# Two heads' scores on the two row halves of TensorE, and softmax reciprocals by transposes, in a fused attention and MLP kernel

## The chip, the cores and the metric

One NeuronCore of a Trainium2 chip runs the whole program. The metric is the device time of one execution in microseconds (us). Both sides are compared by the median of several executions; beside them stands one profiled execution, from which all rows below are read.

## The reference, cut to what matters

```python
def _attn_ref(q, k, v, f):                      # 4 batches, 8 heads, 576 tokens, head size 64, float32
    scores = np.matmul(q, k.transpose(0, 1, 3, 2)) / np.sqrt(D)
    cum = np.cumsum(np.log(np.clip(f, 0.0001, 1.0)), axis=-1)
    decay = cum[:, :, :, None] - cum[:, :, None, :]
    scores = np.where(causal, -1000000000.0, scores + decay)
    attn = np.exp(scores - np.max(scores, axis=-1, keepdims=True))
    attn = attn / (np.sum(attn, axis=-1, keepdims=True) + 1e-09)
    return np.matmul(attn, v)
...
h = x @ w_in        # 2304 tokens, 512 -> 2048, leaky relu, 2048 -> 512
g = np.maximum(0.01 * h, h)
x = g @ w_out       # then a second MLP of the same sizes with silu
```

The term of the gates `f` that differs along a row of scores is the cumulated logarithm of the key's position. So the kernel adds one row per head, the cumulated gates, to the product of queries and keys.

## The kernel before, in words

The host only lays inputs out. Everything is float32. A float32 matmul of TensorE runs in four passes and shows in the trace as two weight loads and two matmul records; where the kernel uses the one-pass type (`F32R`), an operand is split into a high and a low part, and three one-pass products stand in for one.

The tokens of a batch are cut in two halves: the first 256 tokens (the first half) and the other 320. An attention step is one head of one half, 64 in all, numbered `n`: 0 to 31 are the first halves (8 heads of 4 batches, `plain(n)`), 32 to 63 the second halves, which the change doesn't touch. A first half has two blocks of 128 queries; the first sees 128 keys, the second 256.

For a step of a first half, before the change:
- `load_first` (batch 0) and `load_head` (the others) bring queries and keys of two heads into tiles of 65 partitions. 64 are the head's dimensions, the 65th is a row of ones (queries) or of cumulated gates (keys), sent by DMAs of its own (L180, L683). So one four-pass matmul of 65 rows gives score plus gate.
- `score` (L744) takes a PSUM bank for each block and queues the matmul (`product`, L792); VectorE adds the mask and takes the row's extreme (L772), ScalarE takes the exponential and its sum (L815).
- The first two steps (`n < DIRECT`) are another case: a matmul of 64 rows (L783) and then 128-row products with the triangle `tri` (L785), before and after the change.
- `transp` (L858) transposes the probabilities on TensorE (L886) in a bank of the set `sp` (three banks), and VectorE or ScalarE copies them to SBUF (L379, L380).
- `pair_shares` (L846) adds 1e-9 to a pair's four columns of sums and takes reciprocals (L849, L850), one per query. `weigh` (L938) does a pair of heads at once: `spread` (L959) brings the reciprocals along the free dimension with four matmuls, each a column of `st` broadcast to 64 columns of weights against the identity, into the second half of a bank; `factors` copies them out as `xn` (L379 or L380); `product` (L979) multiplies values by probabilities, the two heads on the two column halves of the array (64 columns each), into the first half of the same bank; L999 multiplies the two, and `to_ring` (L920) writes high and low parts into the ring that feeds the first MLP.

The rest of the kernel is the two MLPs. The first product of the first MLP (L1062, tiles `hps`, `hpw`) runs between the attention steps. Its weights come as words which `conv_in` (L1892, `to_f32` L1837) turns into float32 and splits: one pass of ScalarE and three of VectorE (L1846 to L1850), then a copy and a subtraction. From 350 us on there is only MLP work.

The order of instructions on each engine is written by a planner (`Plan`): it simulates the engines with costs given in the code and queues what has the lowest rank first. Attention has rank 0, the first MLP and its weights rank 1. A matmul of the first MLP fills what attention leaves; before there is one, TensorE is given filler products of zeros (`fillers`, L476 to L486). On the chip, each engine runs its queue strictly in this order and waits where an operand is not ready.

## Time and profile before

| what | us |
|---|---|
| median of 3 executions | 945.29 |
| lowest and highest | 942.88, 946.74 |
| the profiled execution, its time | 945.92 |
| its span from first to last instruction | 944.2 |

Of the span, the first halves' attention takes about the first 85 us, the second halves' reaches to some 350 us. PE is TensorE's matmul side, PEld its weight loads, DVE is VectorE, ACT is ScalarE, POOL is GpSimd; SPq is the queue that issues most DMAs. A matmul's record lasts longer than the array is held by it, since ends are modelled and records overlap; what a matmul costs is read from its start to the start of the next one. In a row of the timeline, the first number is the start and the second the length of the merged records, `x2` their count; `65*128 65x256` means 65 rows of weights by 128 columns, against 256 columns that stream through.

### The profile page before, as it was taken

Reading aid. Unit: us, or ns where it says so; the run is one execution under the profiler, and the core shown is the slowest. Engines: PE = TensorE matmul, PEld = TensorE weight load, DVE = VectorE, ACT = ScalarE, POOL = GpSimd, SP = SyncE. Lnnn points to the kernel's source line nnn. Section 1 sums busy time; section 2 is a strip of 40 time slices with the busy share of each in tenths; the row PEclk is TensorE's granted clock in tenths of the full one; section 3 lists DMA queues with packets and bytes.
Section 4 is the critical chain, followed back from the end, with each engine's and each line's share of the span. In section 5 each row is a group of like instructions: output and inputs, shape, how many; then the busy total and the mean of one; then the engine's idle time right before and its main releaser. Section 6 shows DMA issues by size and latency. Waiting matters only on the chain.

```text
span 944.2 us, 17797 instructions
## 1 busy us (share of the span) xinstructions
PE 936.8 (99%) x6389; PEld 882.4 (93%) x6389; DVE 739.4 (78%) x1715; ACT 593.5 (63%) x1301; POOL 72.0 (8%) x79
## 2 busy tenths in 40 slices
PE   9999999999999999999999999999999999999998
PEld 7777997788898989999999999999999999999998
DVE  5889964988898853889889699848564588888885
ACT  6879965676787863666446477556466764444442
POOL 2002331121331200000000000000000000000000
PEclk9999999999999999999999999999999999999999
DMA  7576634778575618996767685896757774454442
GB/s 196 153 194 205 195 106 137 231 232 260 191 241 188 208 57 298 335 382 199 248 239 233 207 266 187 302 332 228 269 175 245 243 224 121 127 156 140 129 135 67
DMA packets 157524, 195.43 MB, mean 207 GB/s; under 512 B 9222, under 2 KB 142966, under 8 KB 157404
## 3 DMA queue, kind: packets, MB, share of 16 engines
q1 hardware_dynamic: 157004, 193.91, 64.1%
q8 instruction: 50, 0.82, 0.4%
q10 hardware_dynamic: 432, 0.39, 0.1%
q14 instruction: 38, 0.31, 0.1%
HBM read 124.61 MB, written 69.65 MB: 206 GB/s over the span
## 4 chain that ended last, share of the span: by engine, by line
PE 89%; DVE 4%; ACT 3%; DMA 2%; issue 1%; SPq 0%; DVEq 0%; ACTq 0%
PE m L1659 19%; PE m L1801 19%; PE acc L1352 16%; PE hpw L1062 14%; PE sps L792 6%; PE av L979 5%; PE hps L1062 4%; PE tps L886 4%; DMA qk<-in_kt_dram 1%; ACT sc L815 1%; DVE gs L394 1%; PE av L959 1%; DMA x_d<-u 1%; DVE gq L1491 1%; DVE sc L772 1%
## 5 line engine op out<-in xcount | busy, mean ns | idle before, releaser
L1352 PE MATMUL acc<-gs,w 128*128 128x384 f32 x1008 | 181.0, 339 | 1.0 <-DVE gs L394 1.0
L1062 PE MATMUL hpw<-ring,w 128*128 128x320 f32 (+1 forms) x960 | 180.7, 330 | 0.0
L1659 PE MATMUL m<-xc,w 128*128 128x384 f32 x1008 | 180.1, 339 | 0.0
L1801 PE MATMUL m<-w,gc 128*128 128x256 f32 x1512 | 179.9, 281 | 0.0
L1801 PEld LDWEIGHTS m<-w,gc 128*128 128x128 f32 x1512 | 179.7, 188 | 0.0
L1352 PEld LDWEIGHTS acc<-gs,w 128*128 128x128 f32 x1008 | 177.7, 188 | 1.5 <-DVE gs L394 1.4
L1659 PEld LDWEIGHTS m<-xc,w 128*128 128x128 f32 x1008 | 177.7, 188 | 0.6 <-ACT z L1697 0.3
L1062 PEld LDWEIGHTS hpw<-ring,w 128*128 128x128 f32 x960 | 150.0, 188 | 6.9 <-issue 0.7
L379 ACT CAST gc<-g 128x512 fp32r<-128x512 f32 (+1 forms) x180 | 80.6, 490 | 85.7 <-DVE g L1491 47.5
L815 ACT ACTIVATE sc<-sc,st 128x576 f32<-128x576 f32 (+2 forms) x160 | 92.8, 581 | 29.3 <-DVE st L772 26.4
L1285 ACT CAST gs<-gq 128x768 fp32r<-128x768 f32 x84 | 69.5, 836 | 46.6 <-PE acc L1352 24.7
L772 DVE CUSTOM_DVE_ANT_0 sc<-sps,zmask 128x288 f32<-128x288 f32 (+2 forms) x160 | 71.7, 450 | 27.7 <-PE sps L792 17.8
L394 DVE TENSOR_TENSOR gc<-g,gc 128x512 fp32r<-128x512 f32 (+1 forms) x180 | 90.4, 528 | 2.7 <-ACT gc L379 1.5
L394 DVE TENSOR_TENSOR gs<-gq,gs 128x768 fp32r<-128x768 f32 x84 | 79.6, 956 | 12.3 <-ACT gs L1285 12.0
L390 POOL TENSOR_TENSOR m<-qk,m 64x288 fp32r<-64x288 f32 x64 | 67.0, 1066 | 256.3 <-ACT m L379 202.3
L1491 DVE TENSOR_TENSOR g<-g 128x256 f32<-128x256 f32 x144 | 58.9, 422 | 18.0 <-DMA g<-g_d 17.3
L2050 ACT CAST w<-w 128x512 fp32r<-128x512 f32 x84 | 50.9, 620 | 30.4 <-DMA w<-w_d 30.1
L886 PE MATMUL tps<-ident,sc 66*107 66x66 f32 (+3 forms) x480 | 66.4, 268 | 0.3
L394 DVE TENSOR_TENSOR w<-w 128x512 fp32r<-128x512 f32 x84 | 56.2, 689 | 12.6 <-ACT w L2050 12.5
L792 PE MATMUL sps<-m,s 66*128 66x288 f32 (+5 forms) x256 | 63.2, 328 | 0.5 <-DVE st L772 0.3
L886 PEld LDWEIGHTS tps<-ident,sc 66*107 66x107 f32 (+3 forms) x480 | 55.4, 152 | 5.5 <-issue 1.8
L1062 PE MATMUL hps<-ring,w 128*128 128x256 f32 x384 | 56.2, 289 | 0.0
(133 smaller groups left out, 1121.5 us busy)
## 6 DMA issues: line engine op xcount, KB each, us to landing
w<-w_d SPq DMA_DIRECT2D x84, 256.0 KB
gq<-g_d SPq DMA_DIRECT2D x48, 384.0 KB
g_d<-z SPq DMA_DIRECT2D x24, 768.0 KB
g<-g_d SPq DMA_DIRECT2D x36, 512.0 KB
w_d<-f SPq DMA_DIRECT2D x16, 896.0 KB
g_d<-gw SPq DMA_DIRECT2D x32, 320.0 KB
qk<-in_kt_dram SPq DMA_DIRECT2D x32, 288.0 KB
wst<-in_w_dram SPq DMA_DIRECT2D x18, 512.0 KB
```

Source lines behind the costliest of these rows:

```text
L379: ("act", act_cost(n, base), lambda: nc.scalar.copy(dst, src), 0.0),
L394: ("dve", dve_cost(n), lambda: nc.vector.tensor_tensor(dst, a, b, op=ALU.subtract), 0.0),
L772: yield dve(w, lambda: nc.vector.tensor_tensor_reduce(out=sc[0:qn, k0:k0 + w], in0=ps[0:qn], in1=zmask[0:qn, z0:z0 + w], scale=-0.125, sca ...
L792: nc.tensor.matmul(ps[0:qn], ht[x][:, qs], ht[y][:, k0:k0 + w], start=r == 0, stop=r == len(ops) - 1)
L815: yield act(kn, lambda: nc.scalar.activation(sc[0:qn, 0:kn], sc[0:qn, 0:kn], ACTF.Exp, scale=-1.0, bias=st[0:qn, col(a):col(a) + 1], accum ...
L886: nc.tensor.transpose(ps[0:k1 - k0, o:o + qn], ht["p"][i][0:qn, k0:k1], ident[0:qn, 0:qn])
L1062: nc.tensor.matmul(dst, w[:, wi, c * 128:(c + 1) * 128], x(xi, c), start=(first_ and c == 0 and r == 0), stop=(c == KC - 1 and r == 2), sk ...
L1285: yield act(2 * TB, lambda: nc.scalar.copy(t[:, 0], src), 0, 0.09)
L1352: nc.tensor.matmul(dst, w[:, e, wi, j * 128:(j + 1) * 128], x[:, xi, e], start=start and s == 0 and e == 0 and r == 0, stop=stop and s == ...
L1491: ("dve", dve_cost(n), lambda: nc.vector.tensor_tensor(dst, a, b, op=op_), 0.0),
L1659: nc.tensor.matmul(dst, w[:, wi, c * 128:(c + 1) * 128], x[:, xi, c], start=start and c == 0 and r == 0, stop=stop and c == 1 and r == 2, ...
L1801: nc.tensor.matmul(banks[b][:, e], t[:, gi, a * 128:(a + 1) * 128], w[:, wi], start=begin and a == 0 and r == 0, stop=jp == NP // 2 - 1 an ...
```

## The change

It concerns the first halves alone, but for one rank.

- **Loads.** Four heads are loaded together: the even ones of the four on partitions 0 to 63, the odd ones on 64 to 127, no 65th row. The cumulated gates get a tile of their own: for batch 0 one float32 row per head on partition 0 or 64 (`first["row"]`), for the others two rows, high and low part (`gate_rows`), read from `cum_d`. The tensor `cum_p` goes, and `cum_d` is sent in two parts.
- **Scores.** `score_pair` queues a block of both heads at once: two matmuls of 64 rows, one on each row half, then two small ones that add the gates, weights of ones on one row (four passes, batch 0) or on two rows (one pass, the other batches). Each head has one bank for both its blocks: the first in columns 0 to 127, the second in 128 to 383. Banks go back when both blocks have been read.
- **Reciprocals.** They are copied 64 times each (`[128, 4, 64]`, ScalarE or VectorE), and `spread` becomes two plain transposes.
- **Weights.** `to_f32` in `conv_in` goes from rank 1 to rank 0. One slot of the weights' store is held until the last first half is scored.

```diff
+    unity = at["const"].tile([128, 128], F32R, name="unity")
...
+    spare = slot(H // 2 - 1, [128, ROW_BUFS, 2, HALF[0][1]], F32R, "gate_rows")
+    gate_rows = [spare[:, i] for i in range(ROW_BUFS)]
...
+            yield dma(221e3, lambda: nc.sync.dma_start(out=cum_d[:, 1:4], in_=f32(cr)), 0)
             signal("cum_d")
+            yield dma(74e3, lambda: nc.sync.dma_start(out=cum_d[:, 0], in_=f32(cr[:, 0])), 0)
+            signal("cum_1")
...
-        yield wait("ones")
-        yield act(256, lambda: nc.scalar.copy(cf[:, 1], ps[0:H]), 0)
+        yield act(256, lambda: nc.scalar.copy(cf, ps[0:H]), 0)
         signal("cf")
+        row = first["row"]
         yield par(*[seq(
-            dma(8e3, partial(nc.sync.dma_start, out=first[i][64:65], in_=cf[2 * i:2 * i + 2]), i - H),
-            signals(("row", i)),
-        ) for i in range(DIRECT // 2, H // 2)])
+            dma(8e3, partial(nc.sync.dma_start, out=row[64 * e:64 * e + 1], in_=cf[e:H:2]), -1),
+        ) for e in range(2)])
...
+            t = slot(i, [128, 2, 2, tn], F32, "qk0")
+
+            def move(e, r, src):
+                dst = t[64 * e:64 * e + 64, :, r]
+                src_ = src[0, 4 * i + e:4 * i + 4:2, 0:64, 0:tn].rearrange("h d s -> d h s")
+                if i == 0 and r and not e:
                     yield op("act", 0.6, lambda: nc.scalar.dma_start(out=dst, in_=src_), 0, 2.0)
...
+            def both(e):
+                if i:
+                    yield wait("cf")
+                yield par(move(e, 0, qt), move(e, 1, kt))
+                if i:
+                    yield wait("rows")
+                for n in range(4 * i + e, 4 * i + 4, 2):
+                    heads[n] = dict(m1=t[64 * e:64 * e + 64, n % 4 // 2, 1], s1=t[64 * e:64 * e + 64, n % 4 // 2, 0],
+                                    c=first["row"][64 * e:64 * e + 1, n // 2], p={}, pt={})
+                    signal(("prep", n))
+
+            yield par(both(0), both(1))
...
+            i_row = yield take("row", ROW_BUFS)
+            rt = gate_rows[i_row % ROW_BUFS]
+
+            def load(dst, src):
+                yield dma(131e3, lambda: nc.sync.dma_start(out=dst, in_=src.rearrange("h d s -> d h s")), 0)
+
+            def row(k):
+                yield wait("cum_d", "gate_rows")
+                yield dma(8e3, lambda: nc.sync.dma_start(
+                    out=f32(rt[64 * k:64 * k + 2]),
+                    in_=cum_d[g + k:g + 4:2, 2:4, t0:ke].rearrange("h c s -> c h s")), 0)
+
+            def side(k):
+                mine = slice(h + k, h + 4, 2)
+                rows = slice(64 * k, 64 * k + 64)
+                yield par(load(k4[rows], kt[b, mine, 0:64, 0:ke]), load(q4[rows], qt[b, mine, 0:64, t0:ke]), row(k))
+
+            yield par(side(0), side(1))
...
+    def score_pair(n):
+
+        two = (n, n + 1)
+        i_st = yield take("st", ST_BUFS)
+        st = stats[i_st % ST_BUFS]
+        p.start(pair_shares(n, st))
+        pss, held = [], []
+        for m in two:
+            ht = heads[m]
+            ht["i_st"] = i_st
+            ht["i_sc", 0] = yield take("sc", SC_BUFS)
+            ht["sc"] = at["sc"].tile([128, S], F32, tag="sc", name="sc")
+        for m in two:
+            name = "h" if n < H and n % 4 else "sp"
+            k = yield take(name, {"h": 2, "sp": 3}[name])
+            pool_, tag, bufs = bank_at(name, k)
+            pss.append(pool_.tile([128, 384], F32, tag=tag, name="sps", bufs=bufs))
+            held.append((name, k))
+        for i, (q0, qn, _, kn) in enumerate(BLOCKS[0]):
+            kn = min(kn, q0 + qn)
+            views = [ps[:, qn * i:qn * i + kn] for ps in pss]
+
+            def product():
+                for ps, m in zip(views, two):
+                    nc.tensor.matmul(
+                        ps, heads[m]["s1"][:, q0:q0 + qn], heads[m]["m1"][:, 0:kn], start=True, stop=False,
+                        skip_group_check=True)
+                for k, (ps, m) in enumerate(zip(views, two)):
+                    c = heads[m]["c"]
+                    ones = unity[64 * k:64 * k + c.shape[0]]
+                    nc.tensor.matmul(
+                        ps, f32(ones) if n < H else ones, c[:, 0:kn], start=False, stop=True, skip_group_check=True)
+
+            yield wait("ones")
+            yield op("pe", pe_cost(kn, 4) + (pe_cost(kn, 4) if n < H else mm_cost(kn)) + 0.1, product, 0, 0.05)
+            for ps, m in zip(views, two):
+                p.start(soften(m, i, ps, st))
+                signal(("scored", m, i))
+        for m, bank_ in zip(two, held):
+            p.start(seq(wait(("min", m, 0, 0), ("min", m, 1, 0)), done_with(*bank_)))
+        ht = heads[n + 1]
+        if "i_qk" in ht:
+            give("qk", ht["i_qk"])
+            give("row", ht["i_row"])
...
+    def soften(n, i, ps, st):
+
+        q0, qn, _, kn = BLOCKS[0][i]
+        kn = min(kn, q0 + qn)
+        ht = heads[n]
+        sc = ht["sc"][:, 256 * i:256 * i + kn]
+        col, total = 2 * i + n % 2, 4 + 2 * i + n % 2
+        yield wait("zmask0")
+        yield dve(kn, lambda: nc.vector.tensor_tensor_reduce(
+            out=sc, in0=ps, in1=zmask[:, ZOFF - q0:ZOFF - q0 + kn], scale=-0.125, scalar=MASK, op0=ALU.add,
+            op1=ALU.min, accum_out=st[:, col:col + 1],
+        ), 0)
+        signal(("min", n, i, 0))
+        yield act(kn, lambda: nc.scalar.activation(
+            sc, sc, ACTF.Exp, scale=-1.0, bias=st[:, col:col + 1], accum_out=st[:, total:total + 1],
+        ), 0, 0.28)
+        signal(("exp", n, i))
+        yield p.after(PE_LAT - LAT)
+        ht["p"][i] = sc
+        signal(("p", n, i))
...
-        yield dve(1, lambda: nc.vector.tensor_scalar(st[:, 4:8], st[:, 4:8], 1e-9, None, op0=ALU.add), 0)
-        yield op("dve", dve_cost(1), lambda: nc.vector.reciprocal(st[:, 8:12], st[:, 4:8]), 0, PE_LAT)
+        yield op("dve", 0.125, lambda: nc.vector.tensor_scalar(st[:, 4:8], st[:, 4:8], 1e-9, None, op0=ALU.add), 0)
+        yield op("dve", 0.125, lambda: nc.vector.reciprocal(st[:, 8:12], st[:, 4:8]), 0)
+        i_x = yield take("xn", XN_BUFS)
+        x = at["const"].tile([128, 4 * D], F32, tag="xn", name="xn", bufs=XN_BUFS)
+        yield copy(
+            4 * D, x.rearrange("p (c d) -> p c d", d=D), st[:, 8:12].unsqueeze(2).broadcast_to([128, 4, D]),
+            "ad", 0, PE_LAT, 0.125, False)
+        give("st", heads[n]["i_st"])
+        factor[n] = x, i_x
         signal(("shares", n))
...
+        x, i_x = (None, None) if half else factor.pop(n - 1)
 
         def spread():
             for i, (q0, qn, _, _) in enumerate(BLOCKS[0]):
-                for e in range(2):
-                    r = st[:, 8 + 2 * i + e:9 + 2 * i + e].broadcast_to([128, D])
-                    nc.tensor.matmul(
-                        ps[64 * e:64 * e + 64, tn + q0:tn + q0 + qn], r, ident, start=True, stop=True,
-                        skip_group_check=True,
-                    )
+                nc.tensor.transpose(ps[:, tn + q0:tn + q0 + qn], x[:, 2 * D * i:2 * D * i + 2 * D], ident)
 
         def factors():
             yield copy(tn, x, ps[:, tn:2 * tn], "ad", 0, None, 0.125, False)
 
         if not half:
-            i_x = yield take("xn", XN_BUFS)
-            x = at["const"].tile([128, tn], F32, tag="xn", name="xn", bufs=XN_BUFS)
-            yield op("pe", 0.5, spread, 0, 0.05)
-            give("st", i_st)
+            yield op("pe", 0.24, spread, 0, 0.05)
...
+            lag = 1 if head_info(n)[1] else 2
+            if DIRECT <= n < PLAIN:
+                if n % 2 == 0:
+                    yield wait(("prep", n), ("prep", n + 1))
+                    yield from score_pair(n)
+                yield wait(("tail", n - lag))
+                p.start(turns(n), lambda n=n: signal(("tail", n)))
+                p.start(weigh(n), lambda n=n: signal(("weighed", n)))
+                continue
...
-        yield from to_f32(t, src, y, t, 1, True)
+        yield from to_f32(t, src, y, t, 0, True)
...
+            if i != H // 2 - 1:
+                give(("w", i), 0)
+        yield wait(("scored", PLAIN - 1, 1))
+        give(("w", H // 2 - 1), 0)
```

## Rows read from the trace of the kernel before

**Rows 1.** The page: busy time of each engine over the span.
```profile
PE 936.8 (99%) x6389; PEld 882.4 (93%) x6389; DVE 739.4 (78%) x1715; ACT 593.5 (63%) x1301; POOL 72.0 (8%) x79
```

**Rows 2.** The page: the chain that ended last, by engine.
```profile
PE 89%; DVE 4%; ACT 3%; DMA 2%; issue 1%; SPq 0%; DVEq 0%; ACTq 0%
```

**Rows 3.** Waits of weight loads: waiter, releaser, us in total, times, longest.
```profile
PEld av L979 <- ACT xn L379: 2.1, 7, 0.4
```

**Rows 4.** Windows: busy us of each engine (instructions), granted clock, DMA share.
```profile
28.00:80.00 52.00, 51.58 (x412) 39.74 (x411) 46.58 (x179) 43.65 (x144) 2.00 (x2) 1.00 0.64 171
```

**Rows 5.** Groups by form: count, busy us, mean ns of one, idle before.
```profile
L959 PE MATMUL av<-ident,st 128*64 128x128 f32 x128 | 10.5, 285 | 0.0
...
L486 PE MATMUL fps<-zmask 128*128 128x128 f32 x34 | 5.7, 277 | 0.0
...
L379 ACT COPY xn<-av 128x256 f32<-128x256 f32 x11 | 4.1, 370 | 4.4 <-PE av L979 2.4 <-PE av L959 2.0
```

**Rows 6.** Timeline of PE, 12 to 18 us.
```profile
12.05 0.39 PE L792 MATMUL sps<-qk 65*128 65x128 f32 x2
12.28 0.39 PE L486 MATMUL fps<-zmask 128*128 128x128 f32 x2
12.50 0.61 PE L792 MATMUL sps<-qk 65*128 65x256 f32 x2
12.95 0.39 PE L486 MATMUL fps<-zmask 128*128 128x128 f32 x2
...
14.38 0.83 PE L486 MATMUL fps<-zmask 128*128 128x128 f32 x6
15.14 0.66 PE L959 MATMUL av<-ident,st 128*64 128x128 f32 x8
15.73 0.49 PE L792 MATMUL sps<-qk 65*128 65x128 f32 x2
16.05 0.49 PE L886 MATMUL tps<-ident,sc 128*128 128x128 f32 x3
```

**Rows 7.** Timeline of PE, 126 to 140 us.
```profile
126.67 13.12 PE L1062 MATMUL hps<-ring,w 128*128 128x256 f32 x108
```

**Rows 8.** Timeline of PE, 48 to 54 us.
```profile
49.68 0.87 PE L979 MATMUL av<-pf,v 128*64 128x256 f32 x8
50.48 0.70 PE L792 MATMUL sps<-k,s 65*128 65x256 f32 x2
51.02 0.49 PE L886 MATMUL tps<-ident,sc 128*128 128x128 f32 x3
51.35 0.39 PE L792 MATMUL sps<-k,s 65*128 65x128 f32 x2
```

**Rows 9.** Timeline of PE, 4.4 to 12.4 us: the first two steps.
```profile
5.88 0.48 PE L783 MATMUL sps<-qk 64*128 64x128 f32 x2
6.29 0.49 PE L785 MATMUL sps<-tri,fs 128*128 128x128 f32 x2
6.71 0.72 PE L522 MATMUL cps<-tri,fs 128*32 128x320 f32 x2
```

**Rows 10.** Timeline of all engines, 36.2 to 37.2 us.
```profile
36.62 0.37 ACT L379 COPY xn<-av 128x256 f32<-128x256 f32 x1
...
37.04 0.20 PEld L979 LDWEIGHTS av<-pf,v 128*64 128x64 f32 x4 [0.24 <-ACT xn L379]
```

**Rows 11.** Timeline of all engines, 29.4 to 31 us.
```profile
30.53 0.37 ACT L379 COPY xn<-av 128x256 f32<-128x256 f32 x1 [1.15 <-PE av L979]
```

**Rows 12.** Timeline of all engines, 13 to 14.2 us.
```profile
13.39 0.39 PE L486 MATMUL fps<-zmask 128*128 128x128 f32 x2
...
13.59 0.29 DVE L772 CUSTOM_DVE_ANT_0 sc<-sps,zmask 128x128 f32<-128x128 f32 x1
```

**Rows 13.** Instructions of the tile `ct`: count, ns, first and last start.
```profile
L394 DVE TENSOR_TENSOR w<-ct,w x16: 654/685/1270, 19.1 to 129.4; 128x512 fp32r<-128x512 f32 x16
```

**Rows 14.** Timeline of the SP queue, 0 to 9 us: DMA issues.
```profile
7.16 0.85 SPq L1884 DMA_DIRECT2D wsr<-in_w_dram  x2
```

More of the change, by code (lines that the diff above doesn't have):

```diff
@@ L24 @@
 XN_BUFS = 2
+ROW_BUFS = 2
 WST_BUFS = 2
@@ L621, in load_first @@
         tn = HALF[0][1]
+        first["row"] = slot(2, [128, H // 2, tn], F32, "row0")
         def group(i):
[L625 to L628 removed]
+            t = slot(i, [128, 2, 2, tn], F32, "qk0")
[3 more added lines that the diff above has]
+                if i == 0 and r and not e:
                     yield op("act", 0.6, lambda: nc.scalar.dma_start(out=dst, in_=src_), 0, 2.0)
@@ L631, in move @@
                     yield dma(131e3, lambda: nc.sync.dma_start(out=dst, in_=src_), 0 if i else -2)
-            if i > 1:
-                yield wait("cf")
-            yield par(move(0, qt), move(1, kt))
-            if 2 * i >= DIRECT:
-                yield wait(("row", i))
-            for n in range(2 * i, 2 * i + 2):
-                heads[n] = dict(m1=t[:, n % 2, 1], s1=t[:, n % 2, 0], p={}, pt={})
-                signal(("prep", n))
+            def both(e):
[9 more added lines that the diff above has]
+            yield par(both(0), both(1))
             yield wait("v0")
-            pair_v[i] = first["v"][:, 2 * i:2 * i + 2], None
-            signal(("values", i))
+            for k in (2 * i, 2 * i + 1):
+                pair_v[k] = first["v"][:, 2 * k:2 * k + 2], None
+                signal(("values", k))
         def values():
@@ L652, in values @@
             signal("v0")
-        yield par(*[group(i) for i in range(H // 2)], values())
+        yield par(*[group(i) for i in range(H // 4)], values())
     def load_head(n):
@@ L671, in values, with four_values @@
             signal(("values", n // 2))
+        def four_values():
+            i_vh = yield take("vh", VH_BUFS)
+            v4 = hd.tile([128, 4, vsrc.shape[3], D], F32, tag="vh", name="v4", bufs=VH_BUFS)
+            yield dma(262e3, lambda: nc.sync.dma_start(out=v4, in_=vsrc[b, h:h + 4].rearrange("h p c d -> p h c d")), 0)
+            for k in range(2):
+                pair_v[n // 2 + k] = v4[:, 2 * k:2 * k + 2], i_vh if k else None
+                signal(("values", n // 2 + k))
         i_qk = yield take("qk", HEAD_BUFS)
@@ L674, in load_head @@
         heads[n] = dict(p={}, pt={}, i_qk=i_qk)
+        if plain(n):
+            p.start(four_values())
+            k4 = hd.tile([128, 2, ke], F32, tag="m1", name="k4")
+            q4 = hd.tile([128, 2, tn], F32, tag="m2", name="q4")
+            i_row = yield take("row", ROW_BUFS)
[12 more added lines that the diff above has]
+            yield par(side(0), side(1))
+            heads[n].pop("i_qk")
+            for k in range(4):
+                m, rows = n + k, slice(64 * (k % 2), 64 * (k % 2) + 64)
+                heads[m] = dict(s1=q4[rows, k // 2], m1=k4[rows, k // 2], c=rt[rows, k // 2], p={}, pt={})
+                if k == 3:
+                    heads[m].update(i_qk=i_qk, i_row=i_row)
+                signal(("prep", m))
+            return
@@ L675, in load_head @@
         if e == 0:
             p.start(values())
-        if plain(n):
-            k2 = hd.tile([65, 2, ke], F32, tag="m1", name="k2")
-            s1 = hd.tile([65, 2, tn], F32, tag="m2", name="s1")
-            two = slice(h, h + 2)
-            def load(dst, src):
-                yield dma(dst.shape[0] * 2 * tn * 4, lambda: nc.sync.dma_start(out=dst, in_=src), 0)
-            def row(dst, src):
-                yield wait("cum_p")
-                yield from load(dst, src)
-            yield par(
-                load(k2[0:64], kt[b, two, 0:64, 0:ke].rearrange("h d s -> d h s")),
-                load(s1[0:64], qt[b, two, 0:64, t0:ke].rearrange("h d s -> d h s")),
-                row(k2[64:65], cum_p[g:g + 2, 1:2, 0:ke].rearrange("g o s -> o g s")),
-                row(s1[64:65], cum_p[g:g + 2, 0:1, t0:ke].rearrange("g o s -> o g s")),
-            )
-            heads[n].pop("i_qk")
-            heads[n + 1] = dict(p={}, pt={}, i_qk=i_qk)
-            for k in range(2):
-                heads[n + k].update(s1=s1[:, k], m1=k2[:, k])
-                signal(("prep", n + k))
-            return
@@ L723, in rows @@
         def rows():
-            yield wait("cum_d")
+            yield wait("cum_d", "cum_1")
             yield dma(4e3, lambda: nc.sync.dma_start(out=f32(s2[64:66]), in_=cum_d[g, 0:2, t0:ke]), 0)
@@ L804, in score @@
                 yield wait("tri", ("logs", 0))
-            cost = pe_cost(w, 4 if plain(n) else 2)
+            cost = pe_cost(w, 4) if plain(n) else mm_cost(w, 2)
             if n < DIRECT:
```

50 lines of the change are left out of this document (23 added, 27 removed).

## The prediction

> **What bounds the kernel now.** I read the page first: TensorE is busy for 936.8 of 944.2 us [rows 1], and the chain that ended last is 89% TensorE [rows 2]. Such a share can hide waits, as records overlap. So I read the waits: the largest that an attention product shows on another engine is 2.1 us in all [rows 3]. Then the windows: from 28 to 80 us TensorE is busy for 51.6 of 52 us, VectorE for 46.6, ScalarE for 43.7, at a granted clock of 1.00, that is 2.4 GHz [rows 4]. From about 28 us on a first-MLP product stands ready when attention has none. Before that TensorE has room: 34 filler records [rows 5], two to a product of 0.22 us (12.28 to 12.50 [rows 6]), make 3.7 us. So after 28 us a microsecond that TensorE gains or loses is one of the end time, and what VectorE or ScalarE gets extra costs only where TensorE comes to wait. I therefore count what the array is held for, from start to start in the timeline.
>
> **Terms from before.** A four-pass score of 65 rows costs 0.23 us for 128 keys and 0.45 for 256 (12.05, 12.28, 12.50, 12.95 [rows 6]); 0.22 and 0.44 in what follows, so a pair of heads costs 2 x 0.66 = 1.32. A one-pass product of 256 columns costs 13.12 / 108 = 0.12 [rows 7], of 128 half that, 0.06. A transpose costs 0.11 (three from 51.02 to 51.35 [rows 8]).
>
> **What a change of shape costs.** The 64-row score of 128 keys starts at 5.88 and its successor at 6.29, the 128-row product after it lasts to 6.71 [rows 9]: 0.41 and 0.42 where 0.22 would do. Each change of the array's shape, into 64 rows and out again, thus costs 0.20. The column halves show of what it is made: three fillers from 14.38 need 0.66, `spread` starts at 15.14, so 0.10 goes before the first instruction of the new shape; the score after it takes 0.32 (15.73 to 16.05) where 0.22 would do, so 0.10 more goes in the first instruction of 128 columns, whose weights can't be loaded ahead [rows 6]. For 64 columns of weights that part is 0.05: `spread` takes 0.59 (15.14 to 15.73), four records long at 0.11 since its eight go in pairs, 0.10 for the change out and 0.05.
>
> **Spread to transposes.** Before: 0.10 + 0.59 + 0.10 in the successor = 0.79, 16 times (128 records, eight each [rows 5]). After: two transposes in the shape that their neighbours have, 0.22. Gain 0.57 x 16 = 9.1 us. The copies of the reciprocals are 16 more of the `xn` form (0.37 us on ScalarE [rows 5], about the same on VectorE), 6 us in all on engines with 5 and 8 us free between 28 and 80 [rows 4]: costed at nothing, hidden behind transposes and copies of probabilities that the pair needs anyway. With that cover gone it is 0.4 on the path of the first four pairs alone, 1.6 us.
>
> **Scores, 15 pairs.** No row shows two row halves at work at once. The nearest are the column halves, whose eight records go in pairs [rows 6], so I take full overlap: 0.22 and 0.44 for a block of both heads. The bound above is that their weight loads, 0.10 each by the first-instruction cost, go one after the other: some 0.5 more per pair. Nor does a row show weights of one or two rows. Shape follows the operand in each dimension (64 rows [rows 9], 64 columns [rows 6], each at the price above), so I take a third shape for the gates, and each block then changes shape three times, 0.60. The bound below is that the gates run in the scores' shape: two changes, 0.40.
> - 12 pairs of batches 1 to 3: (0.22 + 0.06 + 0.60) + (0.44 + 0.12 + 0.60) = 2.04 against 1.32, +0.72, in all +8.6 us.
> - 3 pairs of batch 0, gates in four passes: (0.22 + 0.22 + 0.60) + (0.44 + 0.44 + 0.60) = 2.52, +1.20, in all +3.6 us.
> - Where a block stands beside a value product, which has a shape of its own, one change of 0.20 falls away. Before, scores are such neighbours on about half the sides (50.48 after 49.68 [rows 8]); with half as many score instructions I estimate 8 cases, -1.6 us.
>
> The planner queues the second block only after the first has ended, so another product comes between, as now, and the two don't share a shape.
>
> The Trainium skill, TensorEngine Tiling (Array Packing), section Key Properties, says that changing the tiling mode, not just the tile, drains TensorE. The rows show that for 64 rows and for column halves, and none shows it for 32-row tiles; by the rule the gates' small matmuls are a mode of their own, and the sum stays as it is, while without it the scores would cost 6.0 us less.
>
> **One bank for both blocks.** In the bank of `weigh`, the product's columns and the columns that `xn` is read from are disjoint, yet they never overlap: the product starts when the copy ends (36.62 + 0.37, then 37.04 [rows 10]) or the copy waits 1.15 us for the product [rows 11]. Before, each score block had a bank of its own; now the second block of a head shares one with the first, which VectorE reads. The read starts 0.20 after the block (13.39 to 13.59 [rows 12]) and takes 0.29; the second head's follows. So the second block can start about 0.20 + 2 x 0.30 + 0.05 = 0.85 after the first, and the product between covers 0.33 to 0.44 of it. What is queued behind a waiting block on TensorE is everything else, first-MLP products too. If VectorE's reads are queued behind the second block, VectorE waits instead, and the exponentials of the first block with it. Bounds: 0, and 0.9 a pair (VectorE first busy with something of 0.4), 13.5 us. I take 0.17 a pair, 2.5 us: TensorE lags its plan here (a block is planned at 0.38 and 0.65, and costs 0.88 and 1.16), which gives VectorE time, and a wait of VectorE's costs nothing while it has some 10% free [rows 4].
>
> **Start and rest.** Rank 0 brings the first weights earlier: the first one is ready at 19.1 us, the last at 129.4 [rows 13]; a first-MLP product may then replace fillers. It may also hold up the first eight heads' exponentials. Between -3.7 (all fillers gone) and +3 (a weight's VectorE work put into the chain) I take -1.5. Seven DMAs for four heads where there were ten save SP's time, which TensorE doesn't wait for; that the gate rows now wait for `cum_d`, sent some us after the tensor it replaces, holds the loads of step 8, which have that much room. In SP's queue the gate rows of batch 0 move behind the first two weights' DMAs: 0.85 us of issue [rows 14], and their bytes in front; step 2 wants them at 12.05 [rows 6]. I count up to 1 us of wait for that, inside the +3. The slot kept until the last first half is scored is the last weight's, converted near 129 us [rows 13], long after: nothing.
>
> **Sum.** -9.1 + 8.6 + 3.6 - 1.6 + 2.5 - 1.5 = +2.5 us, on the profiled 945.92 (span 944.2) 948.4. The median is 945.29, 0.6 less, so 948. Within 0.5% (4.7 us, about what a measurement tells from no change), the forecast is no change.
>
> **Rivals.**
> - *Second blocks wait for the bank.* As above, 0.55 a pair on average, a few longer behind VectorE work: 15 x 0.55 = 8.3 in place of 2.5, 954. It decides from 0.3 a pair on. For it: every value product that follows its `xn` copy shows the wait [rows 3, 10]. Against: some 0.4 is covered, and TensorE is late. The Trainium skill, PSUM — Partial Sum Buffer, section PSUM bank collisions, has a rule on this side: guard by bank and quadrant, not by address.
> - *Weight loads of the two row halves go one by one*: 15 x 0.5 = 7.5 us more, 956. Nothing for it but that no row shows the pair; the column halves speak against.
> - *The gates run in the scores' shape*: 30 x 0.20 = 6.0 us less, 942; with the bank waits at nothing 939.5, faster.
> - *Shape changes cost nothing for row halves*, two for one: scores 12 x (0.84 - 1.32) + 0 = -5.8, spread -9.1, others as above but for the -1.6: 931. The 64-row scores [rows 9] speak against. The Trainium skill, TensorEngine Tiling (Array Packing), section Theoretical Speedup, gives up to 2x for a contraction of at most 64 rows, which is this case; rows of one half alone can't show the factor.
>
> **Chances and range.** Forecast 0.42 (own range 943 to 950); bank 0.20; loads 0.10; gates in one shape 0.22, of which 0.14 end under 940.6; free changes 0.06. So faster 0.20, same 0.50, slower 0.30. The range leaves out the free changes, the best of the third and the worst of the first two: 939 to 957.
>
> **What would show it.** In the timeline of the changed kernel: a score block of 64 rows whose records start in pairs (right) or one after the other; 0.10 before and in the first gate record (right) or none; from a block's start to its successor's 0.88 and 1.16 less the 0.10 paid by the neighbours; transposes where `spread` was, 0.22 without a gap; waits of the second block on VectorE's L772 successor, near 2.5 us in total (8 would be the first rival); fewer fillers. The prediction is wrong if the first-MLP products run out between 30 and 90 us, so that TensorE idles, or if a stage after 130 us changes its length.

## The result, and the profile after

The changed kernel takes 952.7 us, against 946.6 us for the kernel before in the same runs: a ratio of 1.0087 (95% interval 1.0059 to 1.0115), slower by 6 to 11 us. The prediction said 948, with 939 to 957 around it and "no change" as the likeliest case. The time lies in the range, off its middle and clear of no change; that it lies there is luck, since the trace shows two large errors of opposite sign.

The page of the changed kernel: busy time over its span of 951.0 us, and the chain that ended last by engine, to be laid beside [rows 1, 2].
```profile
PE 939.3 (99%) x6406; PEld 881.6 (93%) x6406; DVE 740.9 (78%) x1727; ACT 596.4 (63%) x1307; POOL 69.0 (7%) x80
...
PE 87%; DVE 5%; DMA 3%; ACT 3%; issue 1%; SPq 0%; DVEq 0%; ACTq 0%
```
TensorE is at 99% as before, but its idle time, span less busy time, is 11.7 us where it was 7.4. Its groups by form tell more (count, busy us, mean ns of one, idle before):
```profile
L493 PE MATMUL fps<-zmask 128*128 128x128 f32 x74 | 13.7, 310 | 0.0
...
L1068 PE MATMUL av<-ident,xn 128*128 128x128 f32 x32 | 6.3, 278 | 0.3 <-DVE xn L1102 0.3
...
L906 PE MATMUL sps<-gate_rows,unity 64*128 64x128 f32 x24 | 3.7, 302 | 0.0
...
L906 PE MATMUL sps<-row,unity 1*128 1x128 f32 x12 | 1.5, 321 | 0.0
```
The 128 records of the spread [rows 5] are 32 transposes; the fillers of this form are 74 where 34 were [rows 5]; and the gates of batches 1 to 3 run in 64 rows, the scores' shape: their two rows stand in a cleared tile of 64, which I had not seen in the diff. Only batch 0's run in one row.

PE's timeline in batch 0 (start, us, engine, line, operation, count), where [rows 6] stood:
```profile
12.26 0.49 PE L900 MATMUL sps<-qk 64*128 64x128 f32 x4
12.68 0.49 PE L906 MATMUL sps<-row,unity 1*128 1x128 f32 x4
13.10 0.49 PE L493 MATMUL fps<-zmask 128*128 128x128 f32 x2
13.56 0.70 PE L900 MATMUL sps<-qk 64*128 64x256 f32 x4
14.19 0.70 PE L906 MATMUL sps<-row,unity 1*128 1x256 f32 x4
14.82 0.89 PE L998 MATMUL tps<-ident,sc 128*128 128x128 f32 x3
15.50 2.34 PE L493 MATMUL fps<-zmask 128*128 128x128 f32 x10
17.77 0.58 PE L900 MATMUL sps<-qk 64*128 64x128 f32 x2
```
The start of the first pair's value product (L1082; L979 in the kernel before), in the changed kernel and then in the kernel before:
```profile
21.23 0.87 PE L1082 MATMUL av<-pf,v 128*64 128x256 f32 x8
```
```profile
16.50 0.87 PE L979 MATMUL av<-pf,v 128*64 128x256 f32 x8
```
So the chain of the early heads is 4.7 us late with its first pair already. The last of that pair's probabilities are copied by VectorE from 16.98 to 17.52 us, but TensorE's order has both blocks of two further pairs (12.26 to 20.53) and the ten fillers ahead of the product. With the sixteenth pair the lag is 7.0 us (93.9 for 86.9). The lag alone is not the loss: e3 below has that pair at 95.3 us and is shorter by 7.6 us of span, with first-MLP products from 27.4 us on and fewer fillers.

And from 46 us on, where [rows 8] stood:
```profile
46.49 0.60 PE L1173 MATMUL hps<-ring,w 128*128 128x256 f32 x3
...
48.65 0.49 PE L900 MATMUL sps<-k,q 64*128 64x128 f32 x4
48.90 0.31 PE L906 MATMUL sps<-gate_rows,unity 64*128 64x128 f32 x2
49.13 0.62 PE L1173 MATMUL hps<-ring,w 128*128 128x256 f32 x3
49.68 0.70 PE L900 MATMUL sps<-k,q 64*128 64x256 f32 x4
50.03 0.47 PE L906 MATMUL sps<-gate_rows,unity 64*128 64x256 f32 x2
50.43 0.55 PE L998 MATMUL tps<-ident,sc 128*128 128x128 f32 x3
50.82 0.38 PE L1068 MATMUL av<-ident,xn 128*128 128x128 f32 x2
50.95 0.60 PE L1173 MATMUL hps<-ring,w 128*128 128x256 f32 x3
```
Both heads' scores of 128 keys take 0.25 us together (48.65 to 48.90), one head's took 0.23 [rows 6]: the row halves work at once. The row at 46.49 is the first of the first MLP's products. Before, from about 28 us on one stood ready nearly whenever attention had none; here there is none for another 18 us, and fillers stand in their place.

Windows of the changed kernel and then of the kernel before (columns as in [rows 4]):
```profile
10.00:20.00 10.00, 10.00 (x60) 7.13 (x59) 4.24 (x18) 6.48 (x21) 0.00 (x0) 0.83 0.91 217
...
28.00:80.00 52.00, 50.35 (x420) 38.83 (x418) 41.55 (x174) 42.95 (x144) 1.56 (x2) 1.00 0.49 137
```
```profile
10.00:20.00 10.00, 10.00 (x80) 8.23 (x78) 7.88 (x32) 7.87 (x27) 0.00 (x0) 1.00 0.83 204
```
TensorE looks busy in both from 10 to 20 us, but issues 60 records where it issued 80, some of them at a lower granted clock (last section), and VectorE's busy time halves (4.24 for 7.88): it gets the early heads' scores later. From 28 to 80 us TensorE now idles for 1.65 us of 52 [rows 4 has 0.42]. The weights are later too: where [rows 13] has the first ready at 19.1 and the last at 129.4, the tile `ct` now shows
```profile
L398 DVE TENSOR_TENSOR w<-ct,w x16: 658/681/1293, 29.7 to 133.3; 128x512 fp32r<-128x512 f32 x16
```

**Where TensorE's time went.** I charge each matmul from its start to the start of the next and sort by what it is for. "Rest" is the span less the three columns: all other matmuls, the changes of shape that they pay, and TensorE's waits. All kernels of the study stand here, in us; "first product" is the start of the first first-MLP product. Each kernel was timed beside its own runs of the kernel before, whose medians lay between 945.2 and 946.6. The columns are of the profiled execution; that of e3, e7 and e9 was some 2 us faster than the median, that of e12 2 us slower.

| kernel | span | fillers | scores, gates | spread | rest | first product | median (ratio to before, interval) |
|---|---|---|---|---|---|---|---|
| before | 944.2 | 8.1 | 24.7 | 9.4 | 902.0 | 27.9 | |
| changed | 951.0 | 17.0 | 23.6 | 3.1 | 907.3 | 46.5 | 952.7 (1.0087, 1.0059 to 1.0115) |
| e1 | 960.3 | 13.3 | 24.6 | 3.2 | 919.2 | 40.4 | 962.8 (1.0182, 1.0163 to 1.0200) |
| e2 | 947.4 | 14.5 | 23.1 | 2.8 | 906.9 | 28.7 | 949.5 (1.0046, 1.0023 to 1.0069) |
| e3 | 943.4 | 11.5 | 23.3 | 3.5 | 905.1 | 27.4 | 947.1 (1.0024, 1.0012 to 1.0036) |
| e4 | 945.4 | 8.2 | 23.6 | 10.4 | 903.2 | 25.3 | 946.4 (1.0009, 1.0000 to 1.0018) |
| e5 | 940.1 | 9.7 | 22.7 | 3.4 | 904.3 | 27.3 | 941.9 (0.9961, 0.9946 to 0.9976) |
| e6 | 946.7 | 4.9 | 26.4 | 3.7 | 911.7 | 47.3 | 947.4 (1.0024, 1.0007 to 1.0041) |
| e7 | 940.5 | 10.4 | 23.0 | 3.5 | 903.6 | 27.4 | 944.3 (0.9988, 0.9975 to 1.0001) |
| e8 | 950.7 | 12.3 | 24.4 | 9.6 | 904.5 | 43.3 | 952.3 (1.0084, 1.0050 to 1.0119) |
| e9 | 939.6 | 7.0 | 24.7 | 3.6 | 904.3 | 40.9 | 943.8 (0.9981, 0.9971 to 0.9992) |
| e10 | 947.2 | 11.5 | 24.3 | 3.5 | 907.9 | 29.0 | 948.9 (1.0044, 1.0027 to 1.0060) |
| e11 | 937.5 | 7.2 | 24.5 | 3.4 | 902.4 | 25.6 | 939.5 (0.9940, 0.9927 to 0.9953) |
| e12 | 942.7 | 7.3 | 23.9 | 3.7 | 907.8 | 39.1 | 942.2 (0.9966, 0.9944 to 0.9988) |

Changed less before: fillers +8.9, scores and gates -1.1, spread -6.3, rest +5.3, in all +6.8, the difference of the two spans. So scores, gates and spread hold TensorE 7.4 us less, and 14.2 us of fillers and rest are added. The study is about those 14.2.

Some 3.3 of them are the scores' own: the part of a change of shape that falls on the records beside a block. By the medians of the trace, a filler or first-MLP product right ahead of a 64-row block is held 0.09 us longer than elsewhere, a filler or product right behind one 0.10, a transpose 0.06; beside the 65-row scores of before, only the products behind them were, by 0.08. Two fillers between blocks show it: 0.46 us from 13.10 to 13.56, where two took 0.22 at 12.28 [rows 6]. Another 4.3 us is the idle time that TensorE shows more, nearly all of it after 60 us.

### The profile page after: what moved, and what is told of

The parts are those of the page before. It is cut to its first block, busy times and chain, and to the rows that moved or that the text cites. A ratio compares the mean times of both kernels' runs of the same rounds, so it can differ in the third digit from the quotient of the medians.

```text
span 951.0 us, 17810 instructions
## 1 busy us (share of the span) xinstructions
PE 939.3 (99%) x6406; PEld 881.6 (93%) x6406; DVE 740.9 (78%) x1727; ACT 596.4 (63%) x1307; POOL 69.0 (7%) x80
## 4 chain that ended last, share of the span: by engine, by line
PE 87%; DVE 5%; DMA 3%; ACT 3%; issue 1%; SPq 0%; DVEq 0%; ACTq 0%
PE m L1770 19%; PE m L1912 18%; PE acc L1463 17%; PE hpw L1173 14%; PE av L1082 5%; PE tps L998 4%; PE sps L822 4%; PE hps L1173 2%; PE sps L900 2%; DMA w_d<-wf 1%; PE fps L493 1%; DVE sc L802 1%; DMA w<-w_d 1%; PE sps L906 1%; DMA wss<-in_w_dram 1%
## 5 line engine op out<-in xcount | busy, mean ns | idle before, releaser
L394 POOL TENSOR_TENSOR m<-qk,m 64x288 fp32r<-64x288 f32 x64 | 64.1, 1021 | 268.4 <-ACT m L383 161.5
L845 ACT ACTIVATE sc<-sc,st 66x320 f32<-66x320 f32 (+3 forms) x100 | 66.1, 661 | 18.6 <-DVE st L802 17.9
L802 DVE CUSTOM_DVE_ANT_0 sc<-sps,zmask 66x320 f32<-66x320 f32 (+3 forms) x100 | 51.1, 511 | 26.8 <-PE sps L822 18.2
```

Of the source, the lines that this page charges most:

```text
L394: nc.gpsimd.tensor_tensor(dst[:, s_], a[:, s_], b[:, s_], op=ALU.subtract)
L802: yield dve(w, lambda: nc.vector.tensor_tensor_reduce(out=sc[0:qn, k0:k0 + w], in0=ps[0:qn], in1=zmask[0:qn, z0:z0 + w], scale=-0.125, sca ...
L845: yield act(kn, lambda: nc.scalar.activation(sc[0:qn, 0:kn], sc[0:qn, 0:kn], ACTF.Exp, scale=-1.0, bias=st[0:qn, col(a):col(a) + 1], accum ...
```

## The experiments

**Is it the late second weight, and the rank?** Theory A: the change gives the weights' first conversion (`to_f32`) rank 0 and leaves the copy and subtraction that follow at rank 1; the second weight's subtraction then stands behind the third's and fourth's first steps (it starts at 44.6 us, 26.6 before), and the first MLP, which needs it, starts 18 us late. Rival B: the chain of the first eight heads is late by itself. Rival C: the loss is TensorE's waits after 60 us. Three kernels.

e1, the rank undone in the changed kernel:
```diff
-        yield from to_f32(t, src, y, t, 0, True)
+        yield from to_f32(t, src, y, t, 1, True)
```


> The changed kernel with the first weights' to_f32 back at rank 1, all else as changed. Theory A (the loss is at the start: the second weight's copy and subtraction, at rank 1, stand behind rank-0 to_f32 of the third and fourth weights, so the first first-MLP product starts at 46.5 us instead of 27.9 and fillers hold TensorE for 8.9 us more): the second weight is done before 36 us, the first product starts at 30 to 37, fillers fall by 3 to 6 us, the time is 946 to 950. Rival B (the chain of the first eight heads is itself late, by the gates' shape of one row and by two heads' work coming at once): first product and fillers as in the changed kernel, 951 to 954. Rival C (the loss is after 60 us, where TensorE's waits grew by 5 us): no better than 951, and above 954 if the last weights are now later than 133 us.

962.8 us: 10 us slower than the changed kernel. The second weight's subtraction starts at 38.3 us and the first product comes 6 us earlier, but the tile `ct` of e1 shows what is given up:
```profile
L398 DVE TENSOR_TENSOR w<-ct,w x16: 660/685/693, 33.8 to 149.1; 128x512 fp32r<-128x512 f32 x16
```
The last weight is 16 us later than in the changed kernel, and the rest grows by 11.9: from 130 to 140 us TensorE is busy for 6.01 us of 10, and the granted clock is 0.80 there and 0.86 in the ten us behind. The rank isn't the loss; without it the change would be worse. This is the condition that Rival C named; Rival C itself holds for a part, the 4.3 us of idle time above.

e2, the next two steps of the first two weights at rank 0 as well:
```diff
-        yield copy(DM, w[:, 0], t)
-        yield less(DM, w[:, 1], t, f32(w[:, 0]), "d")
+        yield copy(DM, w[:, 0], t, "a", 0 if f in FO[:2] else 1)
+        yield less(DM, w[:, 1], t, f32(w[:, 0]), "d", 0 if f in FO[:2] else 1)
```


> The changed kernel with the copy and the subtraction of the first two weights at rank 0 as well. Theory A: the second weight is done by 30 us, the first first-MLP product starts at 28 to 34 us, fillers fall by 5 to 9 us, the time is 944 to 948. Rival B: the second weight is early, but the first product waits for the first heads' outputs, fillers fall by under 2 us, 951 to 954. Rival C: fillers fall as A says, but TensorE's waits after 60 us take it back, 950 to 953.

949.5 us. The second weight's subtraction starts at 27.9, and PE's timeline has
```profile
28.65 0.60 PE L1173 MATMUL hps<-ring,w 128*128 128x256 f32 x3
```
18 us earlier than after the change, yet the fillers fall by 2.5 us only, and the time by 3.2: attention still feeds TensorE too slowly, and the first products are soon used up. Theory A had 5 to 9 for the fillers. The intervals of e2 and of the changed kernel overlap, so the 3.2 us are not quite settled either.

e4, the kernel before with the rank alone (the line of e1 reversed):

> The kernel before with nothing changed but the first weights' to_f32 at rank 0. Theory A, if the rank alone does it: the second weight is done later than 30 us (26.6 before), the first product starts later than 31 (27.9 before), fillers grow by 3 us or more, 948 to 952. Rivals B and C: the start is as before within 2 us, 944 to 948.

946.4, as before within 0.1%, although the last weight is ready at 98.2 us in place of 129.4. So neither the rank nor the last weight's time bounds the kernel before. **Theory A falls** as the main cause: an early first product brings some 3 us of the 14.2 back (e2), and e9 below is faster than before although its first product comes at 40.9 us.

**The gates' shape, and the order.** e3 gives batch 0's gate rows 64 rows that are zero but for the first:
```diff
+            yield op("pool", 0.9, lambda: nc.gpsimd.memset(first["row"], 0.0), 0)
+            signal("row_zero")
...
+        yield wait("row_zero")
...
-                                    c=first["row"][64 * e:64 * e + 1, n // 2], p={}, pt={})
+                                    c=first["row"][64 * e:64 * e + 64, n // 2], p={}, pt={})
```


> The changed kernel with batch 0's gate rows in 64 rows that are zero but for the first, so that its gates have the scores' shape, as those of batches 1 to 3 have. By the changed kernel's timeline one change of shape of 0.20 per block falls away, 6 x 0.20 = 1.2 us. Theory A: the time falls by about 1.2 us, to 951 to 952, unless the second weight comes earlier too. Rival B (the first heads' chain): the granted clock stays at 1.00 from 10 to 20 us, the first heads come 1 to 3 us earlier, the fillers fall by 3 us or more, 946 to 949.

947.1 us, 5.7 better, far more than the 1.2 of the six changes of shape. But the cleared tile also moves the order of the whole start. e10 takes the last line of that diff back; its instructions stand in the order of e3 on every engine:

> The kernel of the run with batch 0's gates in 64 rows, with the gates' matmuls reading one row again: every engine's order is the same as in that run, and only the shape of twelve gate matmuls differs. If the gain of that run (952.7 to 947.0) comes from the gates' shape, on TensorE and by the granted clock: 950 to 953. If it comes from the order, which the cleared tile moved: 947 to 948.5, that is the 1.2 us of six changes of shape at 0.20 and no more.

948.9 us, 0.4 above the bounds for the order and below those for the shape. PE's timeline of e3 and then of e10, the same block:
```profile
12.52 0.49 PE L903 MATMUL sps<-qk 64*128 64x128 f32 x4
12.84 0.39 PE L909 MATMUL sps<-row,unity 64*128 64x128 f32 x4
13.16 0.49 PE L495 MATMUL fps<-zmask 128*128 128x128 f32 x2
```
```profile
13.01 0.49 PE L903 MATMUL sps<-qk 64*128 64x128 f32 x4
13.43 0.49 PE L909 MATMUL sps<-row,unity 1*128 1x128 f32 x4
13.85 0.49 PE L495 MATMUL fps<-zmask 128*128 128x128 f32 x2
```
0.64 against 0.84: a change of shape costs 0.20, as forecast, and six make 1.2 of the 1.9 us between the two medians, whose intervals overlap. The other 3.8 us of e3's gain, changed kernel to e10, come with one cleared tile and another order, 5.5 us of fillers fewer among them. The start's order, dealt anew by any edit, is worth some us in this kernel. Of all comparisons here only e3 against e10 holds the order fixed; each other carries such a share, and its size is settled no better than that.

**The two halves of the change by themselves.** e5 is the kernel before with the transposes and the rank, scores as before; e8 is the changed kernel with the old spread.
```diff
+        i_x = yield take("xn", XN_BUFS)
+        x = at["const"].tile([128, 4 * D], F32, tag="xn", name="xn", bufs=XN_BUFS)
+        yield copy(
+            4 * D, x.rearrange("p (c d) -> p c d", d=D), st[:, 8:12].unsqueeze(2).broadcast_to([128, 4, D]),
+            "ad", 0, PE_LAT, 0.125, False)
...
-                    nc.tensor.matmul(
-                        ps[64 * e:64 * e + 64, tn + q0:tn + q0 + qn], r, ident, start=True, stop=True,
-                        skip_group_check=True,
-                    )
+                nc.tensor.transpose(ps[:, tn + q0:tn + q0 + qn], x[:, 2 * D * i:2 * D * i + 2 * D], ident)
```


> The kernel before with the reciprocals copied and transposed (the change's second half) and to_f32 at rank 0, scores as before. Theory D (the scores' part brings TensorE little and makes the first 46 us, where VectorE and ScalarE set the pace, longer; the transposes bring theirs after that): TensorE is held 6 us less by the spread, fillers grow by at most 3 us, 938 to 942. Rival E (whatever TensorE saves before 46 us and what the copies of reciprocals add on VectorE and ScalarE goes into fillers and waits, for this half of the change as for the other): 944 to 948.

> The changed kernel with the old spread by eight matmuls in column halves, so with the scores' half of the change alone (and to_f32 at rank 0). By TensorE's hold the spread costs 6 us more and some changes of shape. Theory D: 956 to 960. Rival E (TensorE's hold before 46 us is covered, and the copies of reciprocals load VectorE and ScalarE): half of it hides, 950 to 955.

e5: 941.9, e8: 952.3. Against e4, which has the same rank, the transposes gain 4.6 us and the row halves lose 5.9. Theory D is right in sign for both, and e5 lies at the upper end of its bounds; e8 came 4 us lower than D said, inside Rival E's 950 to 955. With the row halves in place the transposes gain nothing on the median (952.3 to 952.7), although the spread's 6.4 us are gone in that step too: fillers grew by 4.7 and the rest by 2.8.

**Do fillers only fill?** e6 ends them once head 3 is scored:
```diff
+            yield wait(("scored", 3, 1))
+            del p.filler["pe"]
             yield wait(("hid", 0, 0))
-            del p.filler["pe"]
```


> The changed kernel with the fillers ended once head 3 is scored, in place of at the first first-MLP block; the order is planned anew and moves a little. If fillers only fill time in which TensorE has nothing to do, they hold up nothing: the same 950 to 954, with that much idle time before the first-MLP products, and more if the granted clock falls for it. If they are in the way of scores and transposes, the first heads come earlier and it is 944 to 949.

947.4 us, 5.3 better, with the first product as late as in the changed kernel (47.3). 12.1 us of fillers are gone, 4.4 come back as rest and 2.8 in the scores; the latter for this, in e6's windows (the number before the last two is the granted clock):
```profile
16.00:18.00 2.00, 1.92 (x11) 1.31 (x10) 2.00 (x10) 2.00 (x7) 0.00 (x0) 0.64 1.09 220
18.00:20.00 2.00, 2.00 (x10) 0.97 (x8) 1.14 (x3) 0.58 (x3) 0.00 (x0) 0.50 1.15 243
20.00:22.00 2.00, 2.00 (x9) 1.22 (x9) 1.63 (x6) 1.00 (x5) 0.00 (x0) 0.50 0.41 83
```
The heads come earlier without them: the fifth pair's value products start at 39.3 us in place of 42.8, the sixteenth's at 89.4 in place of 93.9. So the fillers seem to have been in the way of scores and transposes, by more than that loss of clock: they are put into TensorE's order where the plan has it idle, and on the chip they can stand in front of work that is ready. Apart from the fillers, TensorE's order is that of the changed kernel up to 29.6 us and another one from there, so a share of the 5.3 may be the new order's.

e7 adds a third buffer for the reciprocals' copies to e3 (`XN_BUFS = 3`), e9 to e7 the end of the fillers at head 7 (as e6, with 7 for 3), and e11 the same to e5.

> The kernel of the run with batch 0's gates in 64 rows, with three buffers for the reciprocals' copies in place of two: since the change such a buffer is held from the exponentials of a pair to its rows in the ring. If two are too few, TensorE's waits from 30 to 100 us fall by 2 us or more, 943 to 945.5; if not, 946 to 948 as without it.

> Batch 0's gates in 64 rows, three buffers for the reciprocals' copies, and the fillers ended once head 7 is scored. If fillers hold up the first heads where TensorE lags the planned order, 3 to 4 us of the 6.3 that they take from 10 to 46 us come back: 940 to 942. If they only fill, or the granted clock falls to 0.5 for some us without them, 943 to 946.

> The kernel before with transposes and to_f32 at rank 0 (the run at 941.9), and the fillers ended once head 7 is scored. Of 6.0 us of fillers from 10 to 46 us 2 to 3 come back if they hold TensorE up: 938.5 to 940.5. If TensorE keeps up with the planned order there, as scores of one head at a time let it, they only fill: 941 to 943.

e7, 944.3: 2.8 below e3 and so within the bounds for "two are too few", but not by the waits that I had named: the rest falls by 1.5 and the fillers by 1.1, and part of it may be the new order. e9, 943.8, as expected if they only fill: the fillers fall by 3.4 us, but scores rise by 1.7 and the rest by 0.7, and the median gains 0.5: there they did little more than fill. e11, 939.5: as expected if they hold TensorE up (or by its order), and the fastest of the study, 0.6% below the kernel before and 1.4% below the changed one. Whether fewer fillers help the kernel before without the transposes was not tried.

**What the row halves are worth at their best.** e9 and e11 have the same transposes, the same rank and as much time in fillers; e9 scores two heads at once and has a third buffer, e11 scores one head after the other. Scores and gates hold TensorE for 24.7 us in e9 and 24.5 in e11, in both some 2.5 us more than their blocks' medians add up to. From this came Theory F: what the halves save, their changes of shape take. e12 issues both blocks of a pair to TensorE in one piece, so that a pair enters and leaves the shape once:
```diff
-            yield op("pe", pe_cost(kn, 4) + (pe_cost(kn, 4) if n < H else mm_cost(kn)) + 0.1, product, 0, 0.05)
+        cost = sum(pe_cost(kn, 4) + (pe_cost(kn, 4) if n < H else mm_cost(kn)) for _, _, kn in spans) + 0.1
+        yield op("pe", cost, product, 0, 0.05)
```


> The kernel at 943.8 (gates of batch 0 in 64 rows, three buffers, fewer fillers) with both blocks of a pair, scores and gates, issued to TensorE in one piece, so that a pair goes into the shape of 64 rows and out of it once and not twice. Theory F (in its best form the row halves save TensorE about 7 us of array time and give 7 us back in changes of shape): some 30 changes fewer at 0.15 to 0.20 are 4 to 6 us, and after what the four reads by VectorE at once cost the time is 939 to 941.5. Rival G (TensorE's waits for VectorE and ScalarE decide, and a pair's work now comes in one burst): 943 to 947.

942.2 us, between the bounds of F and of G; the interval (0.9944 to 0.9988) overlaps e9's (0.9971 to 0.9992), so the median's 1.6 us are not settled. PE's timeline and the largest wait for VectorE's scores have something of both theories:
```profile
45.86 0.49 PE L906 MATMUL sps<-k,q 64*128 64x128 f32 x4
46.10 0.31 PE L912 MATMUL sps<-gate_rows,unity 64*128 64x128 f32 x2
46.25 0.65 PE L906 MATMUL sps<-k,q 64*128 64x256 f32 x4
46.54 0.47 PE L912 MATMUL sps<-gate_rows,unity 64*128 64x256 f32 x2
46.94 0.63 PE L1182 MATMUL hps<-ring,w 128*128 128x256 f32 x3
```
```profile
PEld sps L906 <- DVE st L945: 2.2, 1, 2.2
```
The pair takes 1.08 us (45.86 to 46.94) where the changed kernel's two blocks take 0.48 and 0.75, so scores and gates fall to 23.9; but the rest is 3.5 us above e9's in the profiled executions (e12's was 2.2 us above its median, e9's the fastest of twelve), part of it at a granted clock of 0.79 from 30 to 46 us.

## Why the prediction was right, and where it was wrong

**Right.** *Spread to transposes*, -9.1, in sign and mechanism: the spread falls by 6.3 us here, and from e4 to e5 by 7.0 with 0.9 in the scores beside it; of that 4.6 came through in e5's median, and 6.9 with fewer fillers in e11's. *The price of a change of shape*, 0.20: 0.84 and 1.26 us for batch 0's blocks (12.26 to 13.10, 13.56 to 14.82), which is 1.04 and 1.48 less the 0.10 before and behind, and e3 against e10 isolates it. *Full overlap of the row halves*: 0.25 for both where one takes 0.23, so the rival of weight loads one by one falls. *One bank for both blocks*: the waits for VectorE's reads are
```profile
PEld sps L900 <- DVE st L936: 1.5, 5, 0.6
```
1.5 us in five, where I had 2.5, and the bank rival 8.3; that rival falls. (Before, all scores together waited 2.5 us for such reads, somewhat more than the 2.1 of [rows 3] that I took for the largest wait; the sum does not hang on it.) *Shape changes for nothing*, 931, falls with the 0.20. Of the wait of up to 1 us for batch 0's gate rows nothing shows: their first block starts at 12.26 where [rows 6] has 12.05. The Trainium skill, TensorEngine Tiling (Array Packing), section Key Properties, calls for a drain at each change of mode; these rows agree, one-row gates being a mode of their own at 0.20 more a block. The same page of the Trainium skill, section Theoretical Speedup, gives up to 2x; inside a block the trace agrees (0.25 for two heads), over the pair nothing of it is left (24.7 against 24.5 us in e9 and e11).

**Wrong, the scores' term.** "I take a third shape for the gates": true of 3 pairs and not of 12, where the gate tile has 64 rows. The third rival had this right: its blocks, 0.22 + 0.06 + 0.20 = 0.48 and 0.44 + 0.12 + 0.20 = 0.76 without what falls on the neighbours, were measured at 0.48 and 0.75. The 1.32 a pair of the kernel before was right: the 24.7 us of the table hold also the first pair's scores (2.1) and what scores paid beside `spread`, and in e5, where that is gone, 20.4 us for 15 pairs are 1.36. The column came out at -1.1, and at about +2 with the 3.3 us that its neighbours pay, where the sum had +8.6 + 3.6 - 1.6 = +10.6.

**Wrong, "Start and rest", -1.5.** This is the step that failed in the other direction, and with it "from about 28 us on a first-MLP product stands ready". Fillers cost +8.9 and the rest +5.3, of which the bank is 1.5. I argued that the rank would bring the weights earlier and replace fillers; the first weight came at 29.7 instead of 19.1. I treated TensorE's gains before 46 us as gains of the end time, and costed the copies of reciprocals at nothing. But there, as I read the rows, the chain of the early heads sets the pace, from TensorE through VectorE and ScalarE and back, with fillers in between: it is 4.7 us late by the first pair, behind two pairs' scores and ten fillers. That VectorE waits there for scores, which now come in bursts of a pair, fits its 4.24 us of 10 but was not tested by itself. I had named the sign of it ("if the first-MLP products run out between 30 and 90 us"), but in a single sentence, and gave it neither a price nor a chance. Put side by side in us, the scores were forecast 8.4 too dear, the spread's gain 2.8 too large, and bank, start and rest (+1.0 forecast, 10.9 left of the 14.2) 9.9 too cheap; together that is the 4.3 between the forecast +2.5 and the +6.8 of the spans.

**What made the 14.2 us.** Shown: that the loss comes with the row halves and the order that goes with them (e8 against e4, 5.9), not with the transposes (e5); the neighbours' part of the changes of shape, 3.3; the order of the start (e10, 3.8, in part fillers); one-row gates (e3 against e10, 1.2 by the timeline, 1.9 by the medians). Shown only together with a new order: fillers that hold TensorE (e6, 5.3 us of the median); two buffers for the copies, up to 2.8 (e7). These overlap and can't be added; with three of them mended, e9 is 9.0 us faster than the changed kernel. Not the cause: the rank (e1, e4); and the time of the first product is at most a small part of it (e2, e9). What is left between the medians of e9 and e11, 4.3 us, goes with the row halves and their order; the profiled executions differ by 2.1, of which 1.9 is rest. Open: what of the idle time after 60 us goes back to the late start; and how much of the order is due to the planner's costs, which have a block of batch 0 at 0.53 and 0.97 us where 0.84 and 1.26 were measured, so that it may see TensorE idle and insert fillers; a kernel with corrected costs was not run.

## What to carry to other kernels

Before a gain on the busiest engine is counted, look stage by stage whether that engine waits there under cover of filler work; in such a stage it comes back as more filler. Count the changes of array shape on both sides of a change: two heads at once in row halves saved nothing here, as each block paid twice 0.20 us, in part on the records beside it. And where an order is planned, run the same work in another order before a cause is named: one cleared tile and the order that came with it were worth 3.8 us.

## What the runs showed of the hardware

The granted clock fell without TensorE standing idle by its records (busy 2.00 us of 2.00). In the changed kernel's windows it is (the number before the last two)
```profile
14.00:16.00 2.00, 2.00 (x14) 1.48 (x11) 1.06 (x6) 0.76 (x4) 0.00 (x0) 0.72 0.94 157
16.00:18.00 2.00, 2.00 (x11) 1.77 (x12) 2.00 (x8) 1.90 (x6) 0.00 (x0) 0.50 0.63 171
18.00:20.00 2.00, 2.00 (x16) 1.28 (x16) 0.45 (x2) 0.00 (x0) 0.00 (x0) 0.93 0.94 245
```
so the clock was 1.2 GHz for some 3.4 us (0.28, 0.50 and 0.07 of 2 us each are missing, 1.7 us in all, at half the clock), behind scores of 64 rows and gates of one row from 12.26 to 14.82. Ten filler records take 2.27 us (15.50 to 17.77) that take 1.21 in e3 (15.07 to 16.28). e10, with scores and gates of the same shapes in another order and fewer fillers, holds 1.00 from 12 to 20 us. It differs between executions of one program: of nine of the changed kernel, six, the profiled one among them, had a mean granted clock of 0.998 or more and took 950.1 to 953.6 us, three had 0.993 to 0.996 and took 957.3 to 959.5. What makes it fall in one execution and not in another was not found.
